# q and k of batch 6 and x of batch 5 turned by transposing transfers, in a kernel whose every step is written out in one list

## The chip, the cores and the metric

The kernel runs on one core of a Trainium2 chip. The metric is the device time of one execution in microseconds (us); lower is better. The engines are called as the profile calls them: PE (TensorE, matmuls; PEld is its weight load), DVE (VectorE), ACT (ScalarE), POOL (GpSimd) and SP (SyncE, which here issues every transfer and computes nothing). Sixteen DMA engines carry the transfers.

## What is computed

The input has 8 batches, 8 heads, 576 positions and a head width of 64. Each batch goes through an attention with two parts and then through a mixing layer. Cut to what matters:

```python
factor = 4
q_d, k_d, v_d = (t.reshape(B, H, 144, 4, D).mean(axis=3) for t in (q, k, v))
out_d  = softmax(q_d @ k_d.T / 8) @ v_d                 # 144 x 144 per head
out_up = np.repeat(out_d, 4, axis=2)
mask   = np.abs(pos[:, None] - pos[None, :]) < 4        # a band
out_local = softmax(where(mask, q @ k.T / 8, -1e9)) @ v
x = (out_up + out_local).transpose(0, 2, 1, 3).reshape(B, 576, 512)

theta = x @ w_theta
y  = w_tok_r @ (x * cos(theta)) + w_tok_i @ (x * sin(theta))   # over positions
u  = x + y
out = u + maximum(u @ w_ch, 0)
```

Inputs and output are float32. The kernel computes in bf16 with float32 sums.

## The kernel before

**The order.** One string, `ORDER`, holds some 1190 words. A word names a step by two letters, and behind them stands the place that the step uses: a letter for the engine of a copy or cast (`v` DVE, `a` ACT, `g` POOL), digits for PSUM banks, or one base-36 digit for one of the 16 staging slots `stg` (576 float32 per partition, shared by loads and by the outputs of some transfers). Each kind of step runs through its batches and parts in a fixed sequence, so the word `ev` for the 25th time is always the same piece. After each step, `pin` ties every instruction to the one before it on its engine. So each engine, and SP's list of transfers too, runs in the order of the words, and an instruction that waits holds up all that stand behind it on its engine.

**The steps of one batch**, with the names used below (the batch stands first: `ev600` is batch 6, half 0, k):

- `lk`, `lq` load k and q, four pieces of 288 KB each per batch; `ck`, `cq` cast a piece to bf16 (`k_tm`, `q_tm`; L295). `lv`, `lw` load the two halves of a window of v, `cv` casts it (L396).
- k and q are needed with the head width on the partitions. `tp` turns half of k or q (four heads, 128 x 1152) by nine transposes on PE (L302) into a pair of PSUM banks, and `ev` copies it to `kT` or `qT` (L315). For batches in `QKD`, `dk` does the turning by one transposing transfer from `k_tm` or `q_tm` into a staging slot (L306), and `ev` copies from there (L312).
- `kd`, `qd` average k and q over four positions (L321 on DVE, L329 with L332 or L335 on POOL); `pv`, `vd` do so for v. `sd`, `ed`, `nd`, `xn`, `xd`, `xc` are the pooled attention: scores (L426), exponential (L437), product with v, division, turning, copy.
- `ps`, `ex`, `mk`, `po`, `nm` are the band attention: scores (L482), exponential (L490), the band's mask `pm` (L503, L505), product with v (L515), division (L523, L524). `xt`, `xa` turn it and add the pooled part, which gives `xT`, x with channels on the partitions (L545).
- `th`, `cs` are theta and its cosine and sine for 128 positions (L556; L561 and L562), `tt`, `ct`, `zt` the same for the last 64, and `dz` or `zp` with `zc` turn that end. `zz` multiplies x by cosine and sine into `z`. For that x is needed with positions on the partitions: `xm` turns 128 positions by four transposes on PE (L595) into PSUM, and `zz` reads PSUM (L620). For batches in `XDMA`, `dx` turns a quarter of `xT` by a transposing transfer into two staging slots (L605), four per batch, and `zz` reads those (L615).
- `mx` mixes over positions, nine matmuls of 288 columns (L636), `ua` adds x and gives `uT` (L641). `du` (transfer, L645) or `up`, `uc` (PE and a copy) turn u. `ch` is u @ w_ch (L666), `rl` the final sum into one of five output buffers `osb` (L671), `st` the store (L675). `ut`, `dt`, `ht`, `rt`, `ss`, `sr` do the last 64 positions of two batches together; `rm` and `su` are the second half of the very last piece.

kT, qT, xT, z, uT have two copies each, used by even and odd batches in turn. The weights are loaded and cast, and the two token matrices turned on PE (`wp`, `wc`), in the first 37 us. `wm` words are matmuls on zeros without a reader.

Before the change, `QKD = (7,)` and `XDMA = (6, 7)`. The code that reads them:

```python
def dk(b, i, n, w):
    to = at["dk", b, i, n] = stg[int(w, 36)].bitcast(BF16)
    nc.sync.dma_start_transpose(out=to.rearrange("p (r e) -> p r e", r=WR),
                                in_=tm[n][(2 * b + i) % TM].rearrange("p r x d -> p (r x d)"))

def zz(b, c, w):
    if b in XDMA:
        nc.vector.tensor_tensor(out=z[b % 2][:, 2 * c:2 * c + 2, :].rearrange("p r (k e) -> p r k e", k=2),
                                in0=dxr(b, c).unsqueeze(1).to_broadcast([P, 2, 2, 256]),
```

Of the kernel before, what the change touches and what calls it, by code (L numbers as in the profile page):

```python
# [45 lines left out]
XDMA = (6, 7)  # L46
# [4 lines left out]
QKD = (7,)  # L51
# [6 lines left out]
kcg l10 l11 l12 l13 kcv lk4 lq5 kcg kcv lk6 lk7 c1v c1g wm7e0 t101 c1v c1v t123 e1a e1v cka ckg wm737 tp01 ckg x12 x13  # L58
lq8 x14 x15 cqg cva cva cqg lk9 ckg cva lqa wm717 tp67 evv x14 cqg lqb cqa tp01 cvv evv wm521 tp23 cva pv47 evv qdv
kdg eva lk1 la3 ckg vda qdg wm624 ps01 ps23 kdv wm656 sd67 sd45 ex mkv la6 cag ex lq4 lq2 lk5 ed ed lk8 ckv ps01 lq9  # L60
po23 nm cqg mkg po67 lba ex cba mkg cqa nd45 nd23 cag tp01 nm xn xn po67 po45 nm nm po23 nm eva xd0 lkb tp67 ckg lq7
cka xca la1 eva cqg la0 cag cqg caa ts lb3 lb4 lb5 xt45 xt01 xt23 tp67 lbc lba lb2 lb8 xa lb1 cbg lv7 kdg th4 lw xa
xm5 th0 lv0 lw lv3 lvb xa cbv cbg tt3 cs xm4 th2 zz evv cbg cs wp0 wp1 wp5 cbg cbg ct lw lw th3 wcv ztg cs cbg xm2 xm0
lv8 cbg wcv wcv wp1 zz zp7 tp45 cs qdg wp3 wp6 zz wcv lw zz wcv wcv zca eva wp7 wcv wp1 wca te wp0 wcv ps34 ps56 ex ex
ps12 mx0 lq1 cvg lk2 lka mx7 lqc mx3 qdv cvg ua lk7 ex ua lk0 mkv mkv kdg sd67 po45 nm sd12 lq4 cva lk5 lk9 cvg cvg ed
ed mx0 ua ua lq3 pv67 po45 po23 nm mx0 vda mkg nd67 lk8 nd45 lkb nm xn xn lq6 ckg ckg tp12 mx3 po45 ua lca ua nm cqg
cqg tp67 eva eva xd0 ckg ckg up1 lq7 po23 lvc xcv nm tp45 xt67 cqg mx0 cqg xt23 eva xt45 lv4 qdg kdg uca lw lv0 lw lw
lv3 lv1 lw lw xa xa tp67 cka ts ckg ckg th1 th2 xa th5 lk8 xm4 evv cs cqg xm1 ckv th3 zz tt4 up6 lq6 lqb cs zz tp12
xm7 ua cs ucv ct cs cqg eva te ztv xm6 zz zz mx0 ua tp34 zp7 tp56 ps12 zcv mx7 mx0 ex cvv kdg evv eva lk7 lk9 cvg lk4
# [733 lines left out]
```

## Time and profile before

| what | us |
|---|---|
| median of 3 runs | 233.41 (233.06 to 235.1) |
| the profiled execution | 233.64 |
| its span, first to last instruction | 231.9 |
| mean granted TensorE clock | 0.994 of full speed |

The span leaves 1.74 us of the profiled execution outside. Sums below are made against the span of the profiled execution; its time lies 0.23 us above the median. The busy time of an engine is the time in which at least one of its instructions ran; since matmuls are pipelined, the times of groups of matmuls overlap and add to more than the busy time of PE.

### The profile page before, as it was taken

How to read it: one execution, taken by the hardware profiler on the slowest of the kernel's cores; microseconds unless marked ns; L12 is line 12 of the kernel's file. 1: busy time of each engine (PE TensorE's matmuls, PEld its weight loads, DVE VectorE, ACT ScalarE, POOL GpSimd, SP SyncE). 2: the span in 40 equal slices, each digit the busy share in tenths (PEclk: the TensorE clock that was granted, in tenths of full speed). 3: DMA queues.
4: the chain of work that ended last, by engine and by line, in shares of the span. 5: the costliest groups of instructions: out<-in, count | busy, mean ns of one | idle time of the engine just before them, and what ended most of it. 6: DMA issues, size and time to landing. Idle time of an engine off the chain costs nothing. (4 is left out here: it accounts for less than half of the span.)

```text
span 231.9 us, 9404 instructions
## 1 busy us (share of the span) xinstructions
PE 217.4 (94%) x3943; PEld 152.4 (66%) x3970; DVE 189.0 (81%) x370; ACT 154.0 (66%) x240; POOL 148.0 (64%) x194
## 2 busy tenths in 40 slices
PE   7997799999999999999999999989998999999990
PEld 2475677776878666876776685766655765578640
DVE  6599998999988889889989798797986976576462
ACT  2279999479988899898878997778777034230000
POOL 7679999949997997996967689379912010200000
PEclk9999999999999999999999999999999999999997
DMA  6999889999999899999999976980665375565777
GB/s 203 401 391 357 280 185 256 384 271 171 334 306 156 205 280 313 160 206 254 159 273 330 259 128 173 152 162 10 95 159 91 64 195 130 118 176 156 117 218 244
DMA packets 76795, 49.41 MB, mean 213 GB/s; under 512 B 61136, under 2 KB 61392, under 8 KB 76752
## 3 DMA queue, kind: packets, MB, share of 16 engines
q1 hardware_dynamic: 76752, 48.81, 83.9%
q8 instruction: 31, 0.51, 1.0%
q14 instruction: 12, 0.10, 0.2%
HBM read 33.98 MB, written 9.44 MB: 187 GB/s over the span
## 5 line engine op out<-in xcount | busy, mean ns | idle before, releaser
L636 PE MATMUL PS<-WT,z 128*128 128x288 bf16 x576 | 78.2, 286 | 0.3 <-DVE z L615 0.2
L636 PEld LDWEIGHTS <-z 128*128 128x128 bf16 x576 | 53.9, 98 | 16.5 <-issue 1.3
L641 DVE TENSOR_TENSOR uT<-PS,xT 128x288 bf16<-128x288 f32 x64 | 28.5, 452 | 10.3 <-PE PS L636 9.5
L561 ACT ACTIVATE cs<-PS,pihc 128x512 bf16<-128x512 f32 x32 | 22.1, 689 | 21.2 <-PE PS L556 20.8
L556 PE MATMUL PS<-wth,xT 128*128 128x512 bf16 x116 | 30.6, 379 | 0.9 <-DVE xT L545 0.3
L666 PE MATMUL PS<-wch,uT 128*128 128x512 bf16 (+1 forms) x122 | 29.6, 372 | 1.0 <-issue 0.6
L671 DVE SCALAR_TENSOR_TENSOR osb<-PS,ur 128x512 f32<-128x512 f32 (+1 forms) x33 | 21.9, 670 | 8.9 <-DMA ur<-uT 4.3
L524 DVE TENSOR_TENSOR tmp<-PS,rl 128x512 bf16<-128x512 f32 x40 | 27.7, 691 | 1.4
L490 ACT ACTIVATE pm<-PS 128x1024 bf16<-128x1024 f32 (+1 forms) x24 | 20.5, 880 | 6.6 <-PE PS L482 5.5
L545 DVE TENSOR_TENSOR xT<-PS,xdT 128x928 bf16<-128x928 f32 (+1 forms) x24 | 22.3, 952 | 3.2 <-PE PS L482 1.5
L577 POOL TENSOR_TENSOR zT<-xT,cst 128x512 bf16<-128x512 bf16 x7 | 10.2, 1456 | 22.1 <-ACT cst L574 14.1
L295 POOL CAST k_tm<-st 128x576 bf16<-128x576 f32 x23 | 15.9, 704 | 6.4 <-DMA st<-in_k_dram 6.3
L765 ACT ACT_TABLE_LOAD x15 | 19.2, 1283 | 0.3
L666 PEld LDWEIGHTS <-uT 128*128 128x128 bf16 x132 | 11.9, 98 | 11.2
L329 POOL TENSOR_TENSOR two<-qT 128x576 f32<-128x576 bf16 x14 | 16.5, 1176 | 4.4 <-ACT qT L315 4.2
L562 ACT ACTIVATE cs<-PS 128x512 bf16<-128x512 f32 x32 | 19.1, 597 | 0.0
L295 POOL CAST q_tm<-st 128x576 bf16<-128x576 f32 x24 | 16.8, 715 | 2.1 <-DMA st<-in_q_dram 2.0
L556 PEld LDWEIGHTS <-xT 128*128 128x128 bf16 x128 | 11.4, 98 | 10.3 <-DVE xT L545 0.7
L503 POOL TENSOR_TENSOR pm<-pm,band 128x512 bf16<-128x512 bf16 x16 | 18.1, 1151 | 0.0
L396 POOL CAST v_w<-st 128x512 bf16<-128x512 f32 x21 | 13.0, 642 | 7.6 <-DVE osb L671 7.6
L620 DVE TENSOR_TENSOR z<-PS,cs 128x1024 bf16<-128x1024 bf16 x24 | 15.8, 684 | 1.0 <-issue 0.5
L329 POOL TENSOR_TENSOR two<-kT 128x580 f32<-128x580 bf16 x13 | 15.0, 1151 | 1.5 <-ACT kT L315 0.9
(121 smaller groups left out, 419.3 us busy)
## 6 DMA issues: line engine op xcount, KB each, us to landing
st<-in_k_dram SPq DMA_DIRECT2D x32, 288.0 KB, 6.0
st<-in_q_dram SPq DMA_DIRECT2D x32, 288.0 KB, 6.0
st<-in_v_dram SPq DMA_DIRECT2D x70, 128.0 KB, 5.4
out_dram<-osb SPq DMA_DIRECT2D x31, 256.0 KB, 3.6
out_dram<-osb SPq DMA_DIRECT2D x10, 128.0 KB, 2.8
st<-in_v_dram SPq DMA_DIRECT2D x4, 288.0 KB, 3.7
st<-in_moe_w_tok_r_dram SPq DMA_DIRECT2D x4, 288.0 KB, 4.3
st<-in_moe_w_tok_i_dram SPq DMA_DIRECT2D x4, 288.0 KB, 5.8
```

The costliest lines, as they stand in the source:

```text
L295: COPY[w](out=to, in_=of)
L329: nc.gpsimd.tensor_tensor(out=t, in0=src[:, :, 0:2], in1=src[:, :, 2:4], op=ALU.add)
L490: nc.scalar.activation(out=pm[(3 * b + u) % NPM][:, :, 0:n].rearrange("p e c j w -> p e (c j w)"), in_=at.pop(("ps", b, u))[:, :, 0:4 * W ...
L524: nc.vector.tensor_tensor(out=tmp[(NCH * b + c) % NTMP].rearrange("p g (j d) -> p g j d", d=D), in0=ps[:, :, :, 0:D], in1=r.unsqueeze(3).t ...
L545: nc.vector.tensor_tensor(out=xT[b % 2][:, :, lo:lo + cnt].rearrange("p e (m j) -> p e m j", j=4), in0=at.pop(("xt", b, u))[:, :, 0:cnt].r ...
L556: nc.tensor.matmul(out=ps, lhsT=xT[b % 2][:, dc, P * c:P * c + P], rhs=wth[:, dc, :], start=(dc == 0), stop=(dc == 3))
L561: nc.scalar.activation(out=t[:, 0, :], in_=ps, func=AF.Sin, bias=pihc, scale=1.0)
L636: nc.tensor.matmul(out=ps, lhsT=z[b % 2][:, j, P * dc:P * dc + P], rhs=WT[:, j, cols], start=(j == 0), stop=(j == 8))
L641: nc.vector.tensor_tensor(out=uT[b % 2][:, dc, cols], in0=at.pop(("mx", b, i)), in1=xT[b % 2][:, dc, cols], op=ALU.add)
L666: nc.tensor.matmul(out=ps[:, cols], lhsT=uT[b % 2][:, dc, P * c:P * c + P], rhs=wch[:, dc, cols], start=(dc == 0), stop=(dc == 3))
L671: nc.vector.scalar_tensor_tensor(out=o[:, cols], in0=at["ch", b, c][:, cols], scalar=0.0, in1=ur[b % 2][:, c, cols], op0=ALU.max, op1=ALU.add)
L765: nc.scalar.activation(out=idle, in_=pihc, func=TABLE[kind])
```

## The change

Two tuples grow by one batch each, and the whole list of words is replaced by another. Everything else is the same.

```diff
-XDMA = (6, 7)
+XDMA = (5, 6, 7)
-QKD = (7,)
+QKD = (6, 7)
 ORDER = """
-kcg l10 l11 l12 l13 kcv lk4 lq5 kcg kcv lk6 lk7 c1v c1g wm7e0 t101 c1v c1v t123 e1a e1v cka ckg wm737 tp01 ckg x12 x13
+l10 l11 c1v l12 l13 c1a wm767 t101 kcg kcv e1a c1g c1a lk4 ckv wm774 t101 lk5 ckv wm732 tp23 lq6 lq7 cqg evv lk8 e1a
...
```

So four `tp` words (36 transposes on PE) and four `xm` words (16 transposes) go, and four `dk` and four `dx` words come. All other steps stay, but where they stand, which engine does a cast or copy, and which bank or slot they use is new throughout. Among the words that change engine, counted over the whole list: the casts of k go from 2 to 6 on DVE and from 23 to 19 on POOL; the masks of two windows go from 8 to 5 on DVE and from 8 to 11 on POOL; of the copies `ev`, DVE has 8 in place of 9, ACT 18 in place of 20, POOL 6 in place of 3. The columns of the matmuls on zeros go from 27 x 512 + 1600 to 27 x 512 + 1920.

Three places, in the order of the instructions on one engine. The first is SP's list around the loads of batches 5 and 6 and the first transposing transfers of k and q. `DMA` is a plain transfer, 128x576 a piece of k or q, 64x8x64 half a window of v, `osb` a store. Before:

```order
L287 DMA st<-in_k_dram 128x576 x2
L287 DMA st<-in_q_dram 128x576 x8
L347 DMA st<-in_v_dram 64x8x64
L287 DMA st<-in_k_dram 128x576
L675 DMA out_dram<-osb_120 128x512
L347 DMA st<-in_v_dram 64x8x64
L287 DMA st<-in_k_dram 128x576 x2
L347 DMA st<-in_v_dram 64x8x64 x3
L306 DMA_TRANSPOSE st<-k_tm_76 128x9x128
L704 DMA out_dram<-osb_121 64x512
L306 DMA_TRANSPOSE st<-q_tm_79 128x9x128
```

And now:

```order
L287 DMA st<-in_k_dram 128x576
L287 DMA st<-in_q_dram 128x576 x3
L306 DMA_TRANSPOSE st<-k_tm_74 128x9x128
L347 DMA st<-in_v_dram 64x8x64 x13
L306 DMA_TRANSPOSE st<-q_tm_77 128x9x128
L306 DMA_TRANSPOSE st<-k_tm_75 128x9x128
L306 DMA_TRANSPOSE st<-q_tm_78 128x9x128
L287 DMA st<-in_k_dram 128x576 x2
L347 DMA st<-in_v_dram 64x8x64
L287 DMA st<-in_q_dram 128x576
L347 DMA st<-in_v_dram 64x8x64 x6
```

Before, the first transposing transfer of this kind was batch 7's and stood behind all loads of k and q and nearly all of v; now batch 6's four stand among the loads, the first ahead of 13 halves of v of batches 5 and 6, the other three ahead of pieces of batch 7.

The second is POOL between the last mask of batch 4 and the pooled k of batch 6. L505 and L503 are masks, L329 with L332 or L335 averages, L295 casts, L577 `zt`, L396 casts of v, L312 copies of what a transfer turned. Before:

```order
L505 TENSOR_TENSOR pm_85<-pm_85,band 128x2x256
L396 CAST v_w_71<-st 128x8x64 x3
L295 CAST k_tm_75<-st 128x9x64 x2
L295 CAST q_tm_77<-st 128x9x64 x2
L295 CAST k_tm_76<-st 128x9x64
L503 TENSOR_TENSOR pm_83<-pm_83,band 128x512 x2
L295 CAST k_tm_76<-st 128x9x64
L295 CAST q_tm_78<-st 128x9x64
L396 CAST v_w_70<-st 128x8x64
L329 TENSOR_TENSOR two<-qT_64 128x576
```

And now, from the copy `ev600` on:

```order
L312 COPY kT_62<-st 128x2x576
L503 TENSOR_TENSOR pm_86<-pm_86,band 128x512 x2
L295 CAST q_tm_78<-st 128x9x64
L396 CAST v_w_71<-st 128x8x64
L503 TENSOR_TENSOR pm_83<-pm_83,band 128x512 x2
L505 TENSOR_TENSOR pm_84<-pm_84,band 128x2x256
L312 COPY qT_64<-st 128x1152
L312 COPY kT_62<-st 128x2x576
L312 COPY qT_64<-st 128x1152
L329 TENSOR_TENSOR two<-kT_62 128x580
L332 TENSOR_TENSOR kd_66<-two 128x2x5x29
```

All three masks of batch 5 and all four copies of batch 6's k and q are on POOL now; before it had one of those masks and none of those copies.

The third is SP at the end, where batch 6's outputs are stored and batch 7's u is turned (L645); the number behind `osb` tells which of the five output buffers. Before:

```order
L645 DMA_TRANSPOSE ur_114<-uT_112 128x4x128 x2
L704 DMA out_dram<-osb_119 64x512
L645 DMA_TRANSPOSE ur_114<-uT_112 128x4x128 x2
L675 DMA out_dram<-osb_120 128x512
L690 DMA_TRANSPOSE utr<-ut_116 128x4x128
L675 DMA out_dram<-osb_121 128x512
L675 DMA out_dram<-osb_122 128x512
```

And now:

```order
L675 DMA out_dram<-osb_120 128x512
L645 DMA_TRANSPOSE ur_114<-uT_112 128x4x128 x2
L704 DMA out_dram<-osb_119 64x512
L645 DMA_TRANSPOSE ur_114<-uT_112 128x4x128 x2
L675 DMA out_dram<-osb_121 128x512
L690 DMA_TRANSPOSE utr<-ut_116 128x4x128
L675 DMA out_dram<-osb_122 128x512
```

The store of batch 6's first block (`st60`, buffer 120) stood behind all four turnings of batch 7's u and now stands ahead of them. On PE the matching `ch60` stood behind all of batch 7's mixing and now stands between `mx72` and `mx73`.

76 lines of the change are left out of this document (38 added, 38 removed).

## The prediction

> **What bounds the kernel now.** I read the page's first part, then the span cut into stages, then PE's order of time inside a stage, then the chain that ended last at the tail. The first part gives the span and the engines' busy time:
>
> ```profile
> span 231.9 us, 9404 instructions
> ...
> PE 217.4 (94%) x3943; PEld 152.4 (66%) x3970; DVE 189.0 (81%) x370; ACT 154.0 (66%) x240; POOL 148.0 (64%) x194
> ```
>
> PE is busy for all but 14.5 us. The cut into stages (start and end, length; busy us and instructions of PE, PEld, DVE, ACT, POOL; granted clock, DMA share, GB/s) tells where these are: 36.8 is the first `mx`, 197.5 the first `mx` of batch 6, 226.1 the end of the last matmul.
>
> ```profile
> 0.00:36.80 36.80, 32.01 (x649) 21.81 (x653) 31.34 (x72) 25.98 (x40) 31.55 (x60) 1.00 0.92 297
> 36.80:104.00 67.20, 66.25 (x1406) 49.66 (x1405) 60.11 (x112) 57.85 (x84) 60.76 (x78) 1.00 0.99 255
> 104.00:144.00 40.00, 39.52 (x764) 27.86 (x767) 35.44 (x71) 34.06 (x56) 31.24 (x35) 1.00 1.00 228
> 144.00:176.00 32.00, 30.88 (x621) 20.70 (x623) 25.75 (x48) 25.11 (x40) 19.46 (x19) 1.00 0.75 118
> 176.00:197.50 21.50, 20.43 (x328) 13.46 (x329) 17.13 (x36) 7.03 (x16) 2.88 (x3) 1.00 0.49 117
> 197.50:226.10 28.60, 28.31 (x195) 18.87 (x195) 17.51 (x33) 3.98 (x8) 2.07 (x2) 1.00 0.65 158
> 226.10:231.90 5.80, 0.01 (x1) 0.00 (x0) 1.69 (x4) 0.00 (x0) 0.00 (x0) 0.75 0.73 248
> ```
>
> The head (36.8 us) is a chain of loads, casts and copies: PE idles 4.8 us there and fills more with matmuls on zeros. In the body, 36.8 to 226.1, PE idles 0.95 + 0.48 + 1.12 + 1.07 + 0.29 = 3.9 us of 189.3. The tail, 5.8 us, has no PE. The clock is full in all stages that PE works in. So each us of PE work taken from the body should shorten it, as long as DVE (60.1 of 67.2 us at its fullest) and the others keep up. That the body waits for PE and not the reverse, the waits of DVE show (total us, times, longest):
>
> ```profile
> DVE uT L641 <- PE PS L636: 9.5, 19, 0.9
> ```
>
> **The transposes taken from PE.** Their groups (count, then busy us and mean ns of one), and two pieces of PE's order of time (start, length):
>
> ```profile
> L302 PE MATMUL PS<-ident,k_tm 128*128 128x128 bf16 x126 | 9.3, 219 | 0.5 <-ACT k_tm L295 0.5
> ...
> L595 PE MATMUL PS<-ident,xT 128*128 128x128 bf16 x96 | 7.8, 219 | 0.0
> ```
> ```profile
> 133.83 0.67 PE L302 MATMUL PS<-ident,q_tm 128*128 128x128 bf16 x9
> 134.33 0.44 PE L447 MATMUL PS<-vd,pd 128*72 128x65 bf16 x8
> ```
> ```profile
> 164.88 0.61 PE L595 MATMUL PS<-ident,xT 128*128 128x128 bf16 x8
> 165.32 1.03 PE L556 MATMUL PS<-wth,xT 128*128 128x512 bf16 x4
> ```
>
> 219 ns is the latency of one; the next work starts 0.50 us after nine of them began and 0.44 us after eight, so one takes 55 ns of PE. Four `tp` and four `xm` are 36 + 16 = 52 transposes, 2.9 us. The other end is the groups' busy time by their count, 9.3 / 126 = 74 and 7.8 / 96 = 81 ns: 36 x 74 + 16 x 81 = 4.0 us, too much where neighbours overlap. All 52 lie in the body, where PE has no cover to lose. I take -2.9, ends -4.0 and, if PE's time just becomes waiting, 0.
>
> **The transfers put in their place.** Sizes and time from issue to landing of their kind, SP's time for one issue, and the DMA engines under plain loads and under transposing transfers:
>
> ```profile
> st<-xT SPq DMA_TRANSPOSE x8, 2.5
> ...
> st<-k_tm SPq DMA_TRANSPOSE x2, 5.1
> ```
> ```profile
> 149.52 2.18 SPq L306 DMA_TRANSPOSE st<-q_tm  x1
> ```
> ```profile
> 187.84 1.24 SPq L605 DMA_TRANSPOSE st<-xT  x1
> ```
> ```profile
> 8.00:16.00 8.00, 7.31 (x111) 5.28 (x110) 5.59 (x5) 4.67 (x8) 6.21 (x9) 1.00 1.06 397
> 144.00:152.00 8.00, 7.30 (x205) 5.21 (x201) 6.46 (x10) 6.29 (x11) 4.07 (x5) 1.00 1.19 136
> ```
>
> SP spends 4 x 2.18 + 4 x 1.24 = 13.7 us more on issuing. `dx5` stands behind batch 7's `dk` and ahead of `du4`; `zz5` reads it only after batch 6's `xa`, many DVE steps later, so 4 x 1.24 + 2.5 us are covered. `dk6` is 4 x 128 x 1152 x 2 bytes = 1.18 MB. At 397 / 1.06 = 375 GB/s for a full share it takes 3.1 us of all sixteen engines, at 136 / 1.19 = 114 GB/s 10.3 us. Its stage, 104 to 144, has a DMA share of 1.00, so it pushes back what is queued behind it: 13 halves of v and batch 7's pieces, which also wait whenever `dk600` waits for its casts. Their first readers on the path are batch 5's v for `po5` and batch 7's chain (below); v is asked for before `dk6` needs its last casts, and from 144 on the share is 0.75 and less. I cost it at 0 beyond that chain.
>
> In a sentence of its own: the Trainium skill (Advanced Engine Details and Errata, X-Bar Transpose) says that transposing transfers are as fast as plain ones on this chip; by that `dk6` would cost the 3.1 us end, but the row of 144 to 152 speaks against it here, and the upper end stays in the range.
>
> **Work moved between engines.** The largest moves:
>
> ```profile
> L503 POOL TENSOR_TENSOR pm<-pm,band 128x512 bf16<-128x512 bf16 x16 | 18.1, 1151 | 0.0
> ```
> ```profile
> L505 DVE TENSOR_TENSOR pm<-pm,band 128x1024 bf16<-128x1024 bf16 x8 | 9.0, 1136 | 0.1
> ```
> ```profile
> L312 POOL COPY kT<-st 128x1152 bf16<-128x1152 bf16 x2 | 4.4, 2180 | 3.9 <-DMA st<-k_tm 3.9
> ```
>
> Three masks leave DVE (-3 x 1.14 us) for POOL (+3 x 2 x 1.15), and POOL has three more `ev` (+3 x 2.18): +13.4 us on POOL, less some casts that leave it. POOL is idle for 8.8 us in 104 to 144 and 12.5 us in 144 to 176, which covers it on the sum; after `ev611` the nearest reader is `ps60`. Cover gone, PE would wait at `ps60` or `sd60` by what POOL is late. DVE's sum does not grow. Head: POOL loses two masks and a `zt` there, DVE gains about what it loses, ACT gains two casts and a copy, but its first copy can come earlier, since seven zeros' matmuls stand ahead of it and not fourteen. Before, ACT waited for it:
>
> ```profile
> 9.15 1.12 ACT L379 COPY xT<-PS 128x1152 bf16<-128x1152 bf16 x1 [7.07 <-PE PS L376]
> ```
>
> I take 0 for the head, ends -1.1 and +1.1 (one such copy either way).
>
> **Batch 7's chain.** PE's first score of batch 7, the copy ahead of it, and two waits of POOL:
>
> ```profile
> 159.00 0.46 PE L482 MATMUL PS<-qT,kT 64*64 64x64 bf16 x32
> ```
> ```profile
> 156.06 1.11 DVE qT L312
> ```
> ```profile
> 129.60 0.66 POOL L295 CAST k_tm<-st 128x576 bf16<-128x576 f32 x1 [3.16 <-DMA st<-in_k_dram]
> ```
> ```profile
> 148.75 2.18 POOL L312 COPY kT<-st 128x1152 bf16<-128x1152 bf16 x1 [3.93 <-DMA st<-k_tm]
> ```
>
> The last `ev7` ended at 157.2, 1.8 us before `ps70`. Now it is on POOL, 2.18 - 1.11 = 1.07 us longer, and PE comes 36 x 0.055 = 2.0 us earlier. If the cast that starts the chain doesn't move, PE waits 1.07 + 2.0 - 1.8 = 1.3 us; if it comes 1.3 us earlier, 0. Nothing decides, so +0.6.
>
> **The tail.** The last matmuls and final sums, and the chain's wait for a store:
>
> ```profile
> 223.94 0.69 DVE L671 SCALAR_TENSOR_TENSOR osb<-PS,ur 128x512 f32<-128x512 f32 x1 [0.57 <-DMA out_dram<-osb]
> ...
> 225.08 1.03 PE L695 MATMUL PS<-wch,ut 128*128 128x512 bf16 x4
> 225.68 1.41 DVE L671 SCALAR_TENSOR_TENSOR osb<-PS,ur 128x512 f32<-128x512 f32 x3 [1.05 <-DMA out_dram<-osb]
> 227.11 0.69 DVE L699 SCALAR_TENSOR_TENSOR osb<-PS,utr 128x512 f32<-128x512 f32 x1
> ```
>
> DVE waited 0.57 and 1.05 us for output buffers, because `st60` stood behind four turnings. The last sum started at 227.11, 1.0 us after PE's end at 226.1. With `st60` ahead, the next stores are late by little: -0.7, ends 0 and -0.9.
>
> **Sum.** -2.9 + 0 + 0.6 - 0.7 = -3.0 us. The profiled execution's own 233.64 becomes 230.6; it lies 0.23 above the median, so the median becomes 230.4.
>
> **Rivals.** (1) No gain: the body is a loop of PE, DVE and copies, and PE's 2.9 us turn into waits. For it speak DVE's 60.1 of 67.2 us; against it that DVE waits 9.5 us for `mx` and PE idles 1.4% up to 104. It gives 233.4 - 0.7 = 232.7, up to 234 with `ps70`'s 1.3. The Trainium skill (Perfetto Trace Analysis, Identifying the Most-Contended Engine) calls matmul busy time a bad measure and takes the busy share of weight loads; by that PE stands at 66%, DVE at 81% is the bound, and this rival holds.
> (2) Slower, by one mechanism: `dk6` in the full DMA stage pushes batch 7's pieces back by up to 10.3 us, its `dk7` follow, and PE stands at `ps70`. POOL's 3.16 us wait for a piece of batch 7 at 129.6 says that those land without slack; against it, from there to 159 stand 29 us for a cast, two transfers of 5.1 and copies. With a delay d at `ps70` PE waits 1.3 + d there. For d = 5, half of the upper end, the time is 230.4 - 0.6 + 6.3 = 236.1; slower than before it is from a wait of 3.6 us (d = 2.3) on, by over 1% from 5.9 us (d = 4.6).
> (3) A bigger gain: -4.0 - 0.9 - 1.1 give 227.4.
>
> **Chances.** About 1% (2.3 us) can be told from no change. Forecast (229.2 to 231.6): 0.48; no gain (231.6 to 234): 0.25; slower: 0.14; bigger gain: 0.13. Faster by over 1% is below 231.1: 0.13 and three quarters of the forecast's, 0.49; slower takes the second rival alone, 0.14; the same is the rest, 0.37. The range 228.2 to 234.2 leaves out the second rival and a little of the third.
>
> **What would show it.** PE's busy time near 214.5 with body idle near 4.5 us: right; busy time down and idle up by as much: rival 1. A wait of PE's scores at `ps70` for POOL's copy of q over 3 us: rival 2. In the tail the last sum should start 0.3 us after PE's end, with no wait for a store over 0.5. I am wrong most easily where the new order makes PE wait in the body at a place that I haven't priced.

## The result and the profile after

The changed kernel takes 235.61 us (median of 20 runs, 232.33 to 238.79), the kernel before 232.60 (20 runs, 231.54 to 235.10). The ratio is 1.011, 95% interval 1.0084 to 1.0136: slower by about 1.1%, where I had forecast 230.4 us. The forecast was made against a median of 233.41 us from 3 runs; as a difference it was -3.0 us, and the measured one is +3.0. Repeated beside the experiments it was 1.0127 (1.0066 to 1.0188).

The trace that came with the first result is of a disturbed run (238.06 us), and so are those of lq5_late, x5_on_pe, x5_on_pe2, x5_on_pe_shift70, zz_free, zz_free_shift70 and before_dx5, which are read below for the order and length of steps and not for the time of the whole; the one read here, `again`, is the same kernel at 233.94 us, the fastest of its six, with a span of 232.2 us. The profiled execution of before took 233.64. So this pair of traces shows the places where time goes and comes from, and too little of the loss. The page's first part:

```profile
span 232.2 us, 9360 instructions
...
PE 217.3 (94%) x3920; PEld 150.7 (65%) x3920; DVE 188.0 (81%) x367; ACT 156.4 (67%) x243; POOL 153.3 (66%) x195
```

PE's sum is where it was (217.4), though it has 52 transposes less. The span cut at the same steps in both kernels: the first `mx` of batches 0, 1, 2, 3, 4, 5 and 6, and the end of the last matmul. The columns are those of the prediction's cut. Before:

```profile
0.00:36.80 36.80, 32.01 (x649) 21.81 (x653) 31.34 (x72) 25.98 (x40) 31.55 (x60) 1.00 0.92 297
36.80:60.80 24.00, 23.48 (x456) 17.96 (x449) 21.81 (x40) 19.43 (x30) 20.58 (x28) 1.00 1.03 279
60.80:94.10 33.30, 32.92 (x688) 23.71 (x679) 30.06 (x59) 29.96 (x45) 30.36 (x38) 1.00 0.99 263
94.10:117.40 23.30, 23.14 (x570) 17.08 (x570) 20.84 (x40) 18.81 (x27) 20.96 (x27) 1.00 1.03 192
117.40:144.10 26.70, 26.33 (x489) 18.76 (x479) 22.94 (x47) 23.70 (x38) 20.20 (x24) 1.00 0.93 239
144.10:173.40 29.30, 28.23 (x603) 18.92 (x604) 25.24 (x47) 22.67 (x36) 19.36 (x19) 1.00 0.74 117
173.40:197.50 24.10, 22.97 (x351) 15.23 (x348) 17.54 (x37) 9.46 (x19) 2.88 (x3) 1.00 0.53 117
```

And after:

```profile
0.00:36.90 36.90, 33.02 (x639) 22.71 (x640) 30.97 (x71) 28.11 (x42) 27.52 (x55) 0.95 0.93 300
36.90:59.90 23.00, 22.99 (x488) 17.41 (x484) 20.49 (x40) 20.10 (x32) 21.71 (x29) 1.00 1.02 266
59.90:95.20 35.30, 34.08 (x674) 24.58 (x671) 31.50 (x62) 29.88 (x44) 32.07 (x43) 1.00 0.98 273
95.20:120.50 25.30, 25.30 (x587) 17.75 (x584) 22.15 (x44) 20.63 (x31) 23.90 (x26) 1.00 1.17 223
120.50:144.80 24.30, 24.25 (x495) 16.97 (x488) 21.46 (x41) 19.00 (x33) 22.46 (x22) 1.00 1.02 201
144.80:175.80 31.00, 27.66 (x525) 17.86 (x520) 26.33 (x46) 22.30 (x36) 20.15 (x19) 1.00 0.79 150
175.80:198.30 22.50, 21.25 (x331) 13.88 (x331) 16.58 (x34) 12.79 (x22) 3.94 (x4) 1.00 0.71 148
198.30:227.50 29.20, 28.77 (x213) 19.51 (x211) 17.85 (x34) 3.58 (x8) 1.55 (x2) 1.00 0.66 164
227.50:232.20 4.70, 0.00 (x0) 0.00 (x0) 0.69 (x1) 0.00 (x0) 0.00 (x0) 0.71 0.68 217
```

The order has moved work between the stages, so the single lengths say little; what counts is the difference of length and PE's busy time. The body (36.9 to 227.5) is 190.6 us, 1.3 more than before, and PE idles 6.3 us in it, 2.4 more than before; 3.3 of them lie in the stage that ends with batch 5's first `mx`, which had 1.07. PE's busy time in the body fell from 185.4 to 184.3 us, by 1.1 and not by the 2.9 of the transposes; in the head it rose by 1.0, where the granted clock was lower (0.95). The tail is 4.7 us, 1.1 less. PE's waits over 0.25 us in the body (what waited, for whom; total us, times, longest; "issue" means that the trace names no releaser):

```profile
PE PS L636 <- ACT cs L562: 2.6, 1, 2.6
PE PS L482 <- issue: 1.2, 1, 1.2
PE PS L515 <- DVE osb L671: 0.9, 1, 0.9
PE PS L482 <- POOL qT L312: 0.8, 1, 0.8
PE PS L636 <- DVE osb L699: 0.4, 1, 0.4
PE PS L556 <- DVE xdn L458: 0.3, 1, 0.3
```

The first is `mx50`, the second lies inside `ps32`, the third is `po70`, the fourth `ps70`. Only `ps70` has a term in my sum.

Around `mx50`, from three views of the same trace in order of time (start, length, instruction, and in brackets the idle time before it and its releaser): DVE, ACT and POOL.

```profile
168.64 5.58 DVE L615 TENSOR_TENSOR z<-st,cs 128x1024 bf16<-128x1024 bf16 x4
```
```profile
174.02 0.62 ACT L396 CAST v_w<-st 128x512 bf16<-128x512 f32 x1 [3.88 <-DMA st<-in_v_dram]
174.54 0.68 ACT L561 ACTIVATE cs<-PS,pihc 128x512 bf16<-128x512 f32 x1
```
```profile
168.96 3.17 POOL L503 TENSOR_TENSOR pm<-pm,band 128x512 bf16<-128x512 bf16 x2
172.09 1.59 POOL L329 TENSOR_TENSOR two<-qT 128x576 f32<-128x576 bf16 x1
```

Two things are late together. ACT's `cv73` waits for the second half of a v piece, and `cs60`, `cs61` stand behind it, whose banks `mx50` and `mx51` take. And the four products `zz50` to `zz53`, which `mx50` reads, take 5.58 us. Their group (least, median and largest ns) in the changed kernel, and in the kernel before, where they read x from PSUM:

```profile
L615 DVE TENSOR_TENSOR z<-st,cs x4: 906/1632/1639, 168.6 to 172.6; 128x1024 bf16<-128x1024 bf16 x4
```
```profile
L620 DVE TENSOR_TENSOR z<-PS,cs x4: 681/681/691, 165.8 to 171.7; 128x1024 bf16<-128x1024 bf16 x4
```

### The profile page after: what moved, and what is told of

It reads as the page before. It is cut to its first block, busy times and chain, and to the rows that moved or that the text cites. A ratio compares the mean times of both kernels' runs of the same rounds, so it can differ in the third digit from the quotient of the medians.

```text
span 236.3 us, 9360 instructions
## 1 busy us (share of the span) xinstructions
PE 218.8 (93%) x3920; PEld 150.8 (64%) x3920; DVE 189.4 (80%) x367; ACT 157.1 (66%) x243; POOL 153.6 (65%) x195
## 4 chain that ended last, share of the span: by engine, by line
PE 64%; DMA 8%; DVE 8%; ACT 6%; SPq 5%; issue 4%; POOL 2%; DVEq 0%; ACTq 0%
PE PS L636 21%; PE PS L556 8%; PE PS L666 7%; PE PS L302 6%; DMA st<-in_v_dram 4%; SPq L347 3%; DVE z L615 3%; PE PS L482 3%; PE PS L537 2%; PE PS L515 2%; DMA st<-xT 2%; DMA utr<-ut 2%; PE PS L759 2%; POOL qT L312 2%; PE PS L595 2%
## 5 line engine op out<-in xcount | busy, mean ns | idle before, releaser
L556 PE MATMUL PS<-wth,xT 128*128 128x512 bf16 x128 | 31.8, 379 | 0.4 <-DVE xdn L458 0.4
L666 PE MATMUL PS<-wch,uT 128*128 128x512 bf16 (+1 forms) x132 | 30.8, 373 | 0.0
L503 POOL TENSOR_TENSOR pm<-pm,band 128x512 bf16<-128x512 bf16 x22 | 25.8, 1197 | 0.0
L577 POOL TENSOR_TENSOR zT<-xT,cst 128x512 bf16<-128x512 bf16 x6 | 6.9, 1154 | 21.0 <-ACT cst L574 21.0
L295 POOL CAST q_tm<-st 128x576 bf16<-128x576 f32 x24 | 15.8, 667 | 6.0 <-DMA st<-in_q_dram 5.9
L396 POOL CAST v_w<-st 128x512 bf16<-128x512 f32 x17 | 10.6, 635 | 12.7 <-PE PS L636 7.6
L437 ACT ACTIVATE pd<-PS 128x864 bf16<-128x864 f32 x16 | 14.1, 890 | 5.0 <-PE PS L426 4.8
L329 POOL TENSOR_TENSOR two<-qT 128x576 f32<-128x576 bf16 x13 | 15.4, 1184 | 2.0 <-DVE qT L315 0.9
L329 POOL TENSOR_TENSOR two<-kT 128x580 f32<-128x580 bf16 x14 | 16.2, 1154 | 0.4
L620 DVE TENSOR_TENSOR z<-PS,cs 128x1024 bf16<-128x1024 bf16 x20 | 13.4, 684 | 0.9 <-PE PS L595 0.4
```

What stands on the lines that cost most here:

```text
L329: nc.gpsimd.tensor_tensor(out=t, in0=src[:, :, 0:2], in1=src[:, :, 2:4], op=ALU.add)
L503: EW[w].tensor_tensor(out=t[:, x], in0=t[:, x], in1=m[:, x], op=ALU.mult)
L556: nc.tensor.matmul(out=ps, lhsT=xT[b % 2][:, dc, P * c:P * c + P], rhs=wth[:, dc, :], start=(dc == 0), stop=(dc == 3))
L666: nc.tensor.matmul(out=ps[:, cols], lhsT=uT[b % 2][:, dc, P * c:P * c + P], rhs=wch[:, dc, cols], start=(dc == 0), stop=(dc == 3))
```

## The experiments

The kernels differ from their parent in a few words of the table that sets the order; the diffs show the places with a word or two around them, `-` the parent. Each row gives the ratio to the kernel before, timed on the same chip.

| kernel | parent, edit | ratio | 95% interval |
|---|---|---|---|
| again | the changed kernel itself | 1.0127 | 1.0066 to 1.0188 |
| lw7_early | changed; v pieces ahead of dx5 | 1.0161 | 1.0113 to 1.0209 |
| lq5_late | changed; two loads later | 1.0207 | 1.0133 to 1.0282 |
| x5_on_pe2 | changed; x of batch 5 on PE | 0.9999 | 0.9968 to 1.0030 |
| pool_still | lw7_early; POOL's work beside the products left out | 1.0036 | 0.9994 to 1.0077 |
| zz_free | lw7_early; one mask, one mean to DVE | 1.0192 | 1.0137 to 1.0248 |
| masks_on_dve | lw7_early; two masks, one mean to DVE | 1.0280 | 1.0224 to 1.0336 |
| shift70 | changed; 70 more instructions ahead | 1.0210 | 1.0152 to 1.0267 |
| zz_free_shift70 | both | 1.0241 | 1.0184 to 1.0298 |
| x5_on_pe_shift70 | x5_on_pe2 and shift70 | 0.9976 | 0.9944 to 1.0007 |
| x5_on_pe_shift70_st | the same, stores ahead of dk7 | 1.0041 | 1.0003 to 1.0079 |
| order_alone | changed; both parts on PE | 1.0264 | 1.0218 to 1.0309 |
| before_dx5 | before; dx5 alone | 1.0295 | 1.0237 to 1.0353 |
| before_dx5_b | before_dx5, other slots | 1.0142 | 1.0097 to 1.0188 |
| before_dk6 | before; dk6 alone | 1.0432 | 1.0377 to 1.0487 |
| before_both | before; both | 1.0619 | 1.0568 to 1.0670 |
| before_tail | before; one step of the new tail | 1.0186 | 1.0163 to 1.0209 |

**The changed kernel again.**

> The changed kernel itself, to have its trace in an execution like most of its runs and its time beside the kernel before. All theories: 235 to 236 us, 1.010 to 1.014 of before, span about 233.9 us; PE waits about 3 us for mx50, 1 us for ps70 and 1.5 to 3 us in three places where no releaser is named, and the body (first mx to end of ht3) is some 4 us longer than before's 189.3 us.

1.0127; the waits are those shown above. Its trace is shorter than expected (span 232.2 us, body 190.6).

**Is it the late v piece?** `lw` are the second halves of the v pieces, `dxd` the first transposing transfer of batch 5's x.

```diff
- eva te dxd evg
+ eva te lw lw lw dxd evg
- ex ts lw ua po45
+ ex ts ua po45
- dz kdg lw du cvv
+ dz kdg du cvv
- kdg rl lw st st
+ kdg rl st st
```

> The changed kernel with the second halves of three v pieces of batch 7 (lw72 to lw74) issued ahead of the four transposing transfers dx50 to dx53 in place of behind them. Theory A (the turned x of batch 5 holds SP's queue for 5 us; lw73 comes late, ACT's cv73 waits for it, cs60 and cs61 stand behind cv73 and mx50 needs their bank): the wait of ACT for in_v_dram (4.5 us) goes, PE's wait ahead of mx50 falls from 3.2 us to about 1 us, where zz53 is next, and the time falls by 2.2 us, to 233.4 us. Theory B (mx50 waits for zz53 anyway, since DVE's products from SBUF are slow): the wait is renamed to zz53 and keeps 2.5 to 3 us; time 235 to 235.6 us.

ACT's wait is gone, and nothing is gained (1.0161). PE's longest wait now:

```profile
PE PS L515 <- DVE osb L671: 2.5, 1, 2.5
```

It is `po70`, which needs the bank that DVE's `rl42` sets free, and `rl42` stands on DVE behind the four products, which keep 1.63 us, and behind `rl40`, the first sum after them. `rl40` waited 1.14 us more, for `du43`, the last turning of batch 4's u:

```profile
176.72 0.69 DVE L671 SCALAR_TENSOR_TENSOR osb<-PS,ur 128x512 f32<-128x512 f32 x1 [1.14 <-DMA ur<-uT]
```

On SP, `du43` stands behind `dx5`: from `dx50`'s start at 160.36 us to `du43`'s end at 175.38 SP's issues follow each other with at most 0.11 us between two. So the late piece covered two other delays, the slow products and the late `du43`, and did not cause the loss by itself. Theory A fell; B was right about one of those that are late, not about the place.

**Products from SBUF or from PSUM.** The first form of this kernel put `xm52` and `xm53` ahead of `xa62`, which reads the same banks, so that `xa62` added turned x in place of batch 6's sums and waited 2.9 us for it:

> The changed kernel with x of batch 5 turned by TensorE again (16 transposes into banks 2, 1, 4 and 5, read from PSUM by the four products), all else in the changed order. Theory A (the transfers dx50 to dx53 cost more by SP's lateness and by slow products from SBUF than the 16 transposes): PE's busy time rises by 0.9 us, the products zz50 to zz53 fall from 1.6 to 0.7 us each, cv73 no longer waits for in_v_dram, the wait ahead of mx50 falls below 0.5 us; time 232.8 to 233.6 us. Theory B (the wait ahead of mx50 belongs to the new order, whichever way x is turned): a wait of 2.5 us or more stays, time 236 to 236.5 us.

It gave 1.0123 (1.0058 to 1.0188), and tells nothing. With the two behind `xa62`:

```diff
-XDMA = (5, 6, 7)
+XDMA = (6, 7)
- eva te dxd evg ztg
+ eva te evg ztg
- rl rl dx dx5 dx po23
+ rl rl po23
- ch7 ch0 utg xa zz
+ ch7 ch0 xm2 xm1 utg xa xm4 xm5 zz
```

> The changed kernel with x of batch 5 turned by TensorE again: 16 transposes into banks 2, 1, 4 and 5, the last eight behind xa62, which reads banks 4 and 5 before them. Theory A (what costs the time around mx50 is DVE: its four products with x read from staging took 5.5 us beside POOL's masks and means, where from PSUM they take 2.5 us, and whatever is put right on ACT, PE then waits for DVE): the four products take 2.5 to 2.7 us together, the sum of PE's waits over 0.25 us between 165 and 185 us falls from 3.5 to 4 us to under 1.5 us, PE's work rises by 0.9 us; time 1.5 to 2 us under the changed kernel's, 1.003 to 1.007 of before. Theory B (the new order is short of time there for any way of turning x): PE keeps over 3 us of waits there and the time is that of the changed kernel or 0.9 us above.

```profile
L620 DVE TENSOR_TENSOR z<-PS,cs x4: 681/681/692, 174.1 to 175.9; 128x1024 bf16<-128x1024 bf16 x4
```

Theory A: the products are back at 681 ns with POOL at work all the while, the long wait ahead of `mx50` is gone, and the time is level with before (0.9999). Turning batch 5's x by transfers costs the changed kernel 1.0127 - 0.9999 = 1.3%, 3.0 us (1.4 to 4.5 by the two intervals), although it takes 16 transposes from PE. This kernel takes away the slow products and the four transfers on SP at once.

**Is it POOL?** Words `mkn` and `qdn` are masks and means of batch 7 that are not computed.

```diff
- sr rl mkg qdg rl cs
+ sr rl mkn qdn rl cs
- te ua mkg ztg po01
+ te ua mkn ztg po01
```

> The changed kernel with lw72 to lw74 issued ahead of dx50, and with three pieces of POOL's work left out (the masks mk70 and mk71 and the means qd71 of batch 7 are not computed, so part of batch 7's output is not the reference's). POOL then stands still beside the products zz51 to zz53. Theory A (products from staging are slow only beside POOL): zz51 to zz53 take 0.68 us each in place of 1.63, DVE is 2.8 us earlier behind them, PE's waits between 165 and 185 us fall below 1.5 us, 1.000 to 1.006 of before. Theory B (from staging they are slow there whatever POOL does): 1.5 to 1.63 us each, PE waits 2.5 us or more, time as that of lw7_early.

```profile
L615 DVE TENSOR_TENSOR z<-st,cs x4: 676/796/1092, 167.7 to 170.2; 128x1024 bf16<-128x1024 bf16 x4
```

The same products, from the same staging slots: those beside nothing take 0.68 us, and the 1.09 us one lies beside a cast of POOL. The ratio falls from lw7_early's 1.0161 to 1.0036, by 2.9 us (1.4 to 4.4 by the two intervals). So theory A is shown as to the products: from staging they are slow beside POOL's work and only there.

That this is the whole price of `dx5` is not shown. PE's longest wait is still 1.5 us, again at `po70` for `rl42`, and in this trace the products don't set it: `rl40` waits 1.90 us after the casts behind them. The trace names an `mx` as its releaser, which `rl40` doesn't read; `du43`, which it does read, was issued at 170.85 us, and `du42` landed 2.44 us after its issue, so by my estimate `du43` landed at 173.3, and `rl40` began at 173.40. In `again` the two are level: `du43` landed at 174.51 us, and `rl40` began behind the products and casts at 174.80.

Two attempts to have this in a whole kernel failed. In the first, mask `mk71` moved up into the place that `mk70` had left (3.16 us beside the products), so it told nothing:

```diff
- sr rl mkg qdg rl cs
+ sr rl mkv qdv rl cs
```

> The changed kernel with lw72 to lw74 issued ahead of dx50, and with one mask (mk70) and one set of means (qd71) of batch 7 moved from POOL to DVE, behind the four products of batch 5. Theory A (the products read x from staging in SBUF and run at 1.63 us each only while POOL works in SBUF as well; from 0.68 us where POOL stands still): zz51 to zz53 take 0.7 us each once POOL's kd71 is over, the masks and means cost DVE 0.42 + 1.34 us, PE's waits between 165 and 185 us fall from 3.5 to 4 us to 1 to 1.5 us; time 2 to 2.8 us under the changed kernel's, 1.000 to 1.004 of before. Theory B (the products are slow because their x comes from staging, whatever POOL does): zz51 to zz53 keep 1.4 to 1.6 us, DVE has 1.8 us more work there, and the time is 0 to 2 us above the changed kernel's.

1.0192. In the second, all of it went to DVE behind the products:

```diff
- sr rl mkg qdg rl cs
+ sr rl mkv rl cs
- te ua mkg ztg po01
+ te ua mkv ztg po01
- po23 nm sd67 ed
+ po23 nm qdv sd67 ed
```

> As zz_free, but with both masks of batch 7 that POOL did beside the products (mk70, mk71) and the means qd71 on DVE, behind the products, so that no mask slips in beside them: zz51 to zz53 take 0.68 us each by theory A, and DVE pays 0.68 + 0.68 + 1.35 us later. Theory A: PE's waits between 165 and 185 us fall to 1 to 2 us, no drop of the granted clock behind them, 1.000 to 1.008 of before. Theory B: DVE is late by as much as before plus 2.7 us; 1.015 to 1.03.

The products took 3.13 us together, as theory A has it, but DVE then stood and waited for `du43` as well, PE for `rl42` and for the means on DVE, and the time is 1.0280:

```profile
175.27 0.69 DVE L671 SCALAR_TENSOR_TENSOR osb<-PS,ur 128x512 f32<-128x512 f32 x1 [2.95 <-DMA ur<-uT]
```
```profile
PE PS L515 <- DVE osb L671: 3.1, 1, 3.1
PE PS L426 <- DVE qd L321: 2.6, 1, 2.6
```

**The stall without a releaser.** Moving two loads away from the place:

```diff
- lq4 lq5 lqc lq1 cqa xd1
+ lq4 lq5 cqa xd1
- ucv lve th4 po23
+ ucv lve lqc lq1 th4 po23
```

> The changed kernel with two loads of q for batch 5 (lq50, lq51, 0.6 MB together) issued some 12 us later, behind lv41. Theory A (the stall of 1.66 us in the middle of ps32 is PE waiting for its next 16 KB of instructions, and that transfer started late because SP had put 7 to 8 us of loads ahead of it in the DMA engines): the issue-to-landing time around 74 us falls from 7 to about 5.5 us, the transfer of instructions starts 1 us or more earlier, and the stall falls below 0.5 us; time 234 to 234.6 us if nothing else takes the gain. Theory B (PE runs through short matmuls faster than instructions can come, whatever the loads): the stall keeps 1.4 to 1.7 us at the same instruction; time 235 to 236 us.

Theory B: PE stalled 1.1 us at the same matmul of `ps32`, and the transfer of instructions began no earlier in the program. The time, 1.0207 (238.0 us), is above both ranges. So the count was changed in place of the loads:

```diff
- lk4 ckv wm774 t101 lk5
+ lk4 ckv wm724 wm701 wm701
...
+ wm701 t101 lk5
```

> The changed kernel with five of the warm-up matmuls of 512 columns (a filler in the head that computes nothing of the output) cut into forty of 64: the same work in about the same time, but 70 more instructions on TensorE (each matmul has its weight load) ahead of all the rest. Theory A (TensorE's instructions come in blocks of 256; the next block is asked for when the one before it is entered, takes 1 to 1.5 us, and can be used some 1.4 us after it has come, so a block that is run through in under 4 us stalls at its end; the place of a stall is a matter of counting): the stall of 1.2 to 1.7 us after seven matmuls of ps32 is gone, since the end of that block lies 70 instructions earlier, where the 256 instructions took 4 us or more; no single stall without a releaser above 0.7 us; time 1 to 2.5 us under the changed kernel's, 1.001 to 1.008 of before. Theory B (the stall belongs to ps32 itself, its banks or its operands): it stays at the eighth matmul of ps32, 1.2 us or more; time as the changed kernel's.

Theory A about the stall: it is gone from `ps32`, and the longest of its kind is 0.8 us. The time is not better but worse, 1.0210. PE reached `mx50` earlier and waited longer (in this program lines stand two lower, so L638 is `mx` and L564 `cs`):

```profile
PE PS L638 <- ACT cs L564: 4.3, 1, 4.3
PE PS L539 <- issue: 0.8, 1, 0.8
```

and behind that wait the granted clock fell (PE's busy us first; the clock is the third number from the end):

```profile
174.00:176.00 2.00, 0.00 (x0) 0.00 (x0) 0.39 (x2) 0.72 (x2) 0.26 (x1) 0.98 0.40 99
176.00:178.00 2.00, 0.97 (x5) 0.61 (x5) 1.86 (x3) 2.00 (x5) 1.21 (x2) 0.50 0.94 359
178.00:180.00 2.00, 2.00 (x10) 1.26 (x9) 1.17 (x3) 1.97 (x5) 2.00 (x3) 0.50 0.66 195
180.00:182.00 2.00, 2.00 (x45) 1.16 (x47) 0.39 (x2) 0.20 (x1) 0.73 (x1) 0.50 0.34 72
182.00:184.00 2.00, 2.00 (x45) 1.26 (x35) 1.93 (x6) 0.89 (x1) 0.00 (x0) 0.81 0.32 65
```

> The two edits together, shift70 and zz_free. Where theory A holds for both, the gains add: 3 to 5 us under the changed kernel's time, 0.992 to 1.000 of before, and so level with the kernel before or ahead of it. Where it holds for one, the time is that one's.

1.0241: neither gain appeared. In its trace two products are still beside a mask (1.64 us each), `rl40` waits 2.3 us for `du43` and PE 3.8 us for `rl42`, and two stalls without a releaser, of 1.4 and 1.1 us, stand at other places. On the kernel that has no long wait:

> x5_on_pe2 (x of batch 5 by TensorE again) with the seventy more instructions ahead (shift70). Theory A (the stall in ps32 is a matter of counting, and no wait behind it takes the gain, since without the products from staging PE waits for nothing long): the stall of 1.9 us goes, 0.991 to 0.996 of before. Theory B (the gain is taken by the next wait, as in shift70): 0.998 to 1.005.

0.9976 (0.9944 to 1.0007): PE's longest wait in the body is 0.5 us and no stall is left in `ps32`. It is the best version of this study, by 0.2%, and its interval reaches just past 1, so it isn't shown to beat the kernel before, and it doesn't decide between the two theories. One more edit, three stores ahead of two transposing transfers:

```diff
- mx6 ps45 dk7 dke
+ mx6 ps45 st st st dk7 dke
...
```

> The same with the stores st21 to st23 issued ahead of the transposing transfers dk700 and dk701 in place of behind them. Theory A (DVE's rl30 waits 1.4 us for a buffer whose store stands behind dk700 and dk701 on SP, and PE's po62 waits 1.3 us for DVE): both waits go, a further 0.5 to 1.3 us under x5_on_pe_shift70. Theory B (the store's own time sets it, or batch 7's transfers come late instead and ps70 waits longer): within 0.5 us of x5_on_pe_shift70.

1.0041, a miss: stalls of 1.4 and 1.0 us without a releaser stand in its trace, on L428 (`sd`) and L484 (`ps`; lines stand two lower here too). PE's instructions are the same as in the kernel just told, whose trace has none over 0.25 us.

**The parts alone.** First dx5 in the old order, the transfers issued while SP was idle:

```diff
-XDMA = (6, 7)
+XDMA = (5, 6, 7)
- nd56 xa nd23 tt0
+ nd56 xa dx0 dx dx2 dx nd23 tt0
- kdg th1 xm0 xm7 cs th6 cs xm4 zz zz
+ kdg th1 cs th6 cs zz zz
- sd12 ch3 xm0 ch7 ch4
+ sd12 ch3 ch7 ch4
```

> The kernel before, in its own order, with x of batch 5 alone turned by transposing transfers, into staging slots 0 and 2, issued in the 8 us in which SP stood idle. Theory A (the part itself costs, through products from SBUF beside POOL): the four products zz50 to zz53 rise from 0.7 to between 1.2 and 1.6 us each, those beside POOL's work most, and what PE saves (0.9 us) comes back as waits of PE for z or for what DVE does behind them; 1.000 to 1.008 of before. Theory B (the part is harmless and the new order loses the time): PE's work falls by 0.9 us, no wait is added, 0.994 to 0.998 of before.

1.0295. Half of that was my slots: a load into slot 1, between 0 and 2, waited 5.1 us on SP for the last product, and the u of batch 4 stood behind it. With slots 2 and 3 (`dx2 dx dx3 dx`):

> before_dx5 with the two staging slots of the turned x next to each other (2 and 3) in place of 0 and 2, since slot 1, which lies between 0 and 2, was loaded with a v piece at the time and that load (lv74) waited 5.1 us for the last product, and du42 and du43 stood behind it on SP. Theory A (products beside POOL's masks cost by themselves): zz50 to zz52 keep 1.6 us each, PE waits 2 to 3 us for DVE at batch 6's po, time 1.005 to 1.015 of before. Theory B (the whole loss of before_dx5 was that load's wait): 0.994 to 1.000 of before.

1.0142, theory A. The three products beside POOL's two masks, and the one after them, which took 0.68 us:

```profile
167.33 4.60 DVE L615 TENSOR_TENSOR z<-st,cs 128x1024 bf16<-128x1024 bf16 x3
...
175.38 0.68 DVE L615 TENSOR_TENSOR z<-st,cs 128x1024 bf16<-128x1024 bf16 x1
```
```profile
PE PS L515 <- DVE uT L641: 2.3, 1, 2.3
```

PE's one long wait is for `ua47`, which stands on DVE behind the three products; no sum waits for a late transfer there, so in the old order the slow products make PE wait by themselves. Behind that wait the granted clock was 0.50 for 3.4 us.

Then dk6, with ACT's copies at their old places:

```diff
-QKD = (7,)
+QKD = (6, 7)
- lw lw xm7 zz
+ lw lw dke xm7 zz
- lw ed tp01 sd67 cva
+ lw ed sd67 cva
- ch2 st cva ts
+ ch2 st dkf cva ts
- ts lv6 th5 up6
+ ts lv6 dke th5 up6
- nm th1 tp34 cs ucv
+ nm th1 cs ucv
- ht3 rt tp67 th1 eva
+ ht3 rt th1 eva
- zz ckg dk4 kdv mx0 cqg tp67 nd23
+ zz ckg kdv mx0 cqg dkf dk4 nd23
```

> The kernel before, in its own order, with k and q of batch 6 alone turned by transposing transfers (staging slots e and f), their copies staying on ACT at their old places in its order. Theory A (these 1.18 MB of transfers in a stage where the DMA engines are full hold back others, and copies from staging take 2.2 us on ACT in place of 1.1): ACT and PE wait 2 to 4 us for them between 118 and 145 us, 1.004 to 1.014 of before. Theory B (as my prediction's sum had it: hidden): PE's work falls by 2.0 us, waits rise by under 0.5 us, 0.990 to 0.995 of before.

1.0432, more than theory A's 1.004 to 1.014. ACT stood at the copy `ev601` for its transfer, and PE behind ACT:

```profile
132.62 2.12 ACT L312 COPY qT<-st 128x1152 bf16<-128x1152 bf16 x1 [4.57 <-DMA st<-q_tm]
```
```profile
135.86 1.87 PE L556 MATMUL PS<-wth,xT 128*128 128x512 bf16 x4 [5.39 <-ACT cs L562]
```

The 1.87 us of those four matmuls, 1.03 elsewhere, are the clock again, 0.50 from 134.5 to 141.3 us.

> The kernel before, in its own order, with both parts of the change. Theory A (parts themselves cost): the sum of the two losses, 1.004 to 1.02 of before, like the changed kernel or worse. Theory B (the new order costs): the sum of the two gains, 0.985 to 0.992 of before.

1.0619, under the sum of the two losses (7.3%) and far above theory A's range. And the new order with neither part (of the places where `dk`, `dx`, `ev` and `xm` words change, four are shown):

```diff
-XDMA = (5, 6, 7)
+XDMA = (6, 7)
-QKD = (6, 7)
+QKD = (7,)
- ex zp0 evg
+ ex zp0 tp23 eva
- mx7 nm cva ts
+ mx7 nm tp23 evv cva ts
- lw th4 xa evg
+ lw th4 tp67 xa evv
- th0 xm2 lk3 lkc evg up6 xn xd7 mx4
+ th0 xm2 tp67 lk3 lkc eva xn mx4 up6 xd7
...
```

> The new order without either part: x of batch 5 and k and q of batch 6 turned by TensorE (36 + 16 transposes put back, their copies on ACT and DVE from PSUM, in banks that the new order leaves free). Theory A (the parts cost in the old order, 3.0 and 4.3%, and the new order is what carries them; dk6 is paid for in it): the time is that of x5_on_pe2 plus at most the 2.0 us of PE's work, 1.000 to 1.009 of before. Theory B (dk6 costs in the new order too, through POOL's slow copies and full DMA engines): 0.990 to 0.998 of before.

1.0264, above both theories' ranges. The stage from batch 3's first `mx` to batch 4's took 28.9 us (24.3 in `again`), with PE idle for 2.6 of them, in waits of 0.3 to 0.7 us for copies and banks around the transposes that I put back. So it doesn't tell what dk6 earns in the new order by itself; that stays open.

**The tail alone.** `ch60`, `rl60` and `st60` ahead of the last turnings, in the old order:

```diff
- mx7 mx4 ua ua ua sr mx7
+ mx7 mx4 ch0 ua ua ua rl sr st mx7
- du ua ch7 ch6 ss ch5 rl rl
+ du ua ch6 ss ch5 rl
- du du st uta dt
+ du du uta dt
```

> The kernel before with one thing of the new order's tail: ch60, rl60 and the store st60 are put ahead of the four turnings of the last batch (du70 to du73), as the new order has them. The tail's term of my prediction says: DVE no longer waits 0.57 and 1.05 us for output buffers, and the last stores end 0.7 to 1.1 us earlier; 0.995 to 0.997 of before. The rival (the last stores are one queue of SP and DMA whose length doesn't change): the waits go, but the time from the last matmul to the end stays 5.8 us; 0.999 to 1.001 of before.

1.0186, a miss on both sides. In its trace `rl60`, 1.5 us late for `ch60`, held `st60` on SP and with it the four turnings; `rl70` then waited 2.4 us for `ur`. The tail grew from 5.8 to 7.8 us, which is 2.0 of the 4.3 us; the rest I can't place. One step of a tail can't be had without the others.

## Why the prediction was wrong, point by point

**The failed step** is in the part on the transfers: "`zz5` reads it only after batch 6's `xa`, many DVE steps later, so 4 x 1.24 + 2.5 us are covered." The transfers of `dx5` themselves were covered: the last landed at 164.85 us and `zz50` began at 168.64. But `dx5` stands in the sum at nothing, and two things about it were left out.

The first is that the four products changed their operand. From PSUM they take 0.68 us beside a busy POOL, from staging 1.63, and POOL's mask beside them (two instructions) 3.17 in place of 2.3. The prediction's own cut showed what should have made me ask: products from staging had so far run only in batches 6 and 7, where POOL works 2.9 and 2.1 us in a whole stage, and batch 5's move into a stage where it works 19.5.

The second is what stands behind `dx5` on SP. The prediction counts the 4 x 1.24 us of issuing and says that `du4` stands behind, but gives that no price. In `again` `cv73` waited 3.88 us for its v piece, and in lw7_early, masks_on_dve and, by the estimate above, pool_still `rl40` waited 1.1 to 3.0 us for `du43`.

The term is not 0 but 3.0 us (x5_on_pe2, 1.4 to 4.5), though it spares 0.9 us of transposes. How it divides between the two is not shown: no kernel here moves `dx5` or `du43` on SP and leaves the products as they are. Of the 6.0 us between the forecast difference and the measured one, the forecast's 0.9 and these 3.0 are `dx5`'s; the other 2.1 are told under dk6 below and have no shown cause.

The Trainium skill (GPSIMD Engine Reference, Specifications) says that GpSimd's SBUF interfaces are shared with VectorE and that they contend with its instructions that have two SBUF inputs. That is what changed here, from one SBUF input to two, and the runs agree: 0.68 against 1.63 us beside POOL's work.

**The transposes**, -2.9: right for the transposes themselves. From each matmul's start to the next one's, summed over the body, `again` has 2.04 us less on L302 (180 to 144 matmuls) and 1.10 less on L595 (80 to 64): -3.1 us. PE's busy time in the body fell by 1.1 us alone, so 2.0 of it came back in other matmuls; I have not followed where, and some records of matmuls are missing in both traces.

**dk6, at 0**: open in the new order. With it and without dx5 the time is 0.9999. By my own terms that kernel should have gained 2.1 us (2.0 of transposes and 0.7 of tail, less 0.6 of wait), more than its interval of 0.3% either way allows, so here too something in the new order costs about 2 us that my sum has at nothing. Its trace has the wait for `ps70` (0.7), 1.3 us at `po62` and the stall of 1.9 in `ps32`. In the old order dk6 cost 4.3%; rival 2 saw a price, but put it at `ps70`, where it was at `ev601`, on ACT.

**Batch 7's chain**, +0.6 (0 to 1.3): right, 0.8 us, for POOL's copy of q.

**The tail**, -0.7 (0 to -0.9): 4.7 us in place of 5.8, -1.1, a little past its end. The mechanism was right: the last sums wait 0.2 us each and no store is late. before_tail shows that it needs the rest of the new tail too.

**What would show it**: PE's busy time is 217.3 us and not near 214.5, and the body's idle time 6.3 and not near 4.5.

**Rival 1**, that the gain becomes waits, was nearest in kind: PE's waits went up by 2.4 us in the body of the best execution. But the new waits are not the old loop's; two of them, the stall in `ps32` and the wait ahead of `mx50`, come from places that I said I hadn't priced.

**What is left open**: the median run is 1.7 us longer than the one whose trace I read. Stalls without a releaser, of 0.3 to 1.9 us at changing places in the traces of its relatives, are candidates, and so is a stretch at half clock; no trace of a median run of the changed kernel was taken that would tell.

## What to carry to other kernels

When a transfer takes a transpose's place, price the reader too: here the products on DVE went from 0.68 to 1.63 us when x moved from PSUM to SBUF and POOL worked beside them. Price also what stands behind the transfers on the engine that issues them. Before a wait is mended, ask what is late right behind it; here the late v piece, the slow products and the late turning of u stood close behind each other, and taking the v piece's delay away gained nothing. And hand-fitted steps of one tuned order don't carry over to another: each part alone that I put into the old order cost 1.4 to 4.3%.

## What the runs showed that I had not expected

**PE stalls for its own instructions.** Transfers of 16 KB, 256 instructions, run on a queue of their own. In `again` PE began a block at 73.89 us, the next one's transfer began at 75.45, took 0.93, and PE went on at 77.87, 1.49 us after its end; the pause of 1.2 us fell between two matmuls of `ps32` that wait for nothing:

```profile
76.42 0.23 PE L482 MATMUL PS<-qT,kT 64*64 64x64 bf16 x7
77.87 0.26 PE L482 MATMUL PS<-qT,kT 64*64 64x64 bf16 x9 [1.22 <-issue]
```

PE had run through the block in 2.8 us. In the kernel before the same block took 4.6 us and the next one's transfer ended 1.77 us before it was needed. So a block of short matmuls can be over before the next one can be used, and seventy instructions ahead (shift70) moved its end elsewhere. A short block doesn't always stall: in `again` another of 2.8 us, by the count of records from 123.03 us on, didn't; the next one's transfer began 0.2 us into it, against 1.56 us here. The Trainium skill (Runtime: NRT & Kernel Launch, Instruction fetch mechanics) gives the 16 KB blocks and calls the cost of crossing one mostly hidden; here it was 0.7 to 1.9 us in `ps32` in each of the ten traces in which the same instructions stand ahead of it.

**A long wait of PE can cost more than itself.** Behind waits of 2.3 to 5.4 us in the body the granted clock was 0.50 for about 3.4 us or for about 6.8 us, which costs up to 1.7 or 3.4 us of PE's work: for the longer time in shift70 (wait 4.3 us, half clock from 175.9 to 182.8), before_dk6 (5.4) and masks_on_dve (3.1), for the shorter in lw7_early (2.5) and before_dx5_b (2.3). It isn't a matter of the wait's length alone: in `again` a wait of 2.6 us was not followed by half clock, nor one of 3.2 in the first trace of the changed kernel, while in before_both one of 1.9 was. The 0.95 in `again`'s first row is such a stretch too, from 21 to 25 us behind three waits of 0.3 to 0.7; it seems to have cost nothing, since the first `mx` began at 36.88 us, before at 36.79.
